# The second of four dense products of an attention and feed-forward kernel, recast as seven block products

## The chip, the cores and the metric

The kernel runs on one core of a Trainium2 chip. The core has TensorE (PE, matrix products; its weight loads are a row of their own, PEld), VectorE (DVE), ScalarE (ACT), GpSimd (POOL) and SyncE (SP). SP and POOL also issue transfers, which 16 DMA engines carry out; POOL issues the ones that add to what stands at the destination. Work data lie in SBUF (128 partitions), matmul results in PSUM (8 banks, a bank holding 128 x 512 fp32). Each engine runs its own list of instructions in order, and waits where an operand or a buffer is not ready. The metric is device microseconds of one execution; the median of several runs counts.

## The reference

Two sequences (B = 2) of 448 tokens (S), 12 heads of 64. First capped attention:

```python
scores = scale * np.matmul(q, k.transpose(0, 1, 3, 2))
scores = cap * np.tanh(scores / cap)
...
attn = attn / (np.sum(attn, axis=-1, keepdims=True) + 1e-09)
return np.matmul(attn, v).astype(np.float32)
```

Its 896 x 768 result goes through two feed-forward stages, each of two dense products (768 to 2048 and 2048 to 768), the first with `g = h * np.cos(h)`, the second with `g = h * (1.0 / (1.0 + np.exp(-h)))`:

```python
h = x @ w_in
g = h * np.cos(h)
return (g @ w_out).astype(np.float32)
```

So there are four dense products: in 1, out 1, in 2, out 2.

## The kernel before, in words

**Precision.** Every fp32 operand of a dense product is split into a high and a low fp32r part; a product of two is three matmuls (high x high, high x low, low x high, `three`). All matmuls have 448 columns. The split of a tile is one copy on ACT (high part) and one subtraction on DVE (low part): `split`. Weights arrive as 64-bit words and are turned into fp32 by two instructions on ACT and two on DVE (`convert`); some of the early ones by one on ACT and three on DVE (`w_abs`, `w_bits`).

**Attention** (to L437) runs pair by pair of heads, its order written out by hand.

**In 1** (`gemm_in`, L542) runs over 16 chunks of the 2048 features, its order also written out by hand. For each chunk TensorE does 36 matmuls (6 blocks of 128 x 3 x 2 sequences). `cos_unit` (L518) computes h cos h with ACT and DVE and at once splits g into `gh` and `gl`, which stay in SBUF until out 1 has read them.

**Out 1** (`gemm_out`, L828) is a plain product: 6 output blocks x 2 sequences x 16 chunks x 3 = 576 matmuls. Its weights come in 18 pieces of 5 or 6 blocks (`cuts`), each converted, split and used once for each sequence. Behind each output block stand the combinations T1 to T4 which in 2 needs.

**In 2** (`gemm_sums`, L898) and **out 2** (`gemm_last`, L1030) are already computed as seven block products each: the operands are cut in 2 x 2 blocks, and seven products of block sums replace the eight of the plain way. That is 504 matmuls each. In in 2 the sums of weight blocks (`sums`) are made on DVE for the first four of eight block rows (p = 0 to 3), and by accumulating transfers for the other four (L913). In out 2 the weight sums are accumulating transfers (`gather`, L1052), and the sums of g run on DVE (`sum_g`).

**The scheduler.** Out 1, in 2 and out 2 are lists of tasks (`do`, with a cost, the buffers that it reads and writes, and a due time). `run_plan` (L653) places them before the kernel is built, each engine taking the ready task with the earliest deadline for which the buffers are free; what comes out is a fixed order of instructions for each engine. Buffers are few: a ring of 8 tiles for split weights, 5 double tiles, 8 PSUM banks, and some 37 half tiles of 128 x 896.

Of the kernel before, what the change touches and what calls it, by code (L numbers as in the profile page):

```python
# [38 lines left out]
def tile_attention_ffn_ffn(  # L39
# [72 lines left out]
    cuts = [(0, 6), (6, 11), (11, KF)]  # L112
    wjobs = []
    for w_in, w_out in ((w_in1, w_out1), (w_in2, w_out2)):
        wi, wo = w_in.bitcast(I32), w_out.bitcast(I32)
        for n in range(KF):
            fc = n if w_out is w_out1 else n // 2 + n % 2 * HP
            wjobs.append((KD, wi[fc]))
        if w_out is w_out1:
            for dm in range(KD):  # L120
                for k0, k1 in cuts:
                    wjobs.append((k1 - k0, wo[dm][:, 2 * P * k0:2 * P * k1]))
        else:
            for n in range(4 * (HK + 1)):
                wjobs.append((KD, wo[n]))
# [63 lines left out]
    with ExitStack() as actx:  # L189
# [144 lines left out]
        def recip(p):  # L334
# [6 lines left out]
            eng = nc.sync if p < NPT - 1 else nc.scalar  # L341
            eng.dma_start(d.rearrange("h (a n) -> (h a) n", a=16), s[:, 0])
            r = ap2.tile([P, S], F32, tag="rb", name=f"rb{p}", bufs=4)
            for u in range(2):
                eng.dma_start(r[u * D:(u + 1) * D, :], d[1 - u:2 - u].to_broadcast([D, S]))
            rb[p] = r

        def norm_mul(p):
            if p < 0:
                return  # L350
            nc.vector.tensor_tensor(out=rb[p], in0=xu.pop(p), in1=rb[p], op=ALU.mult)
# [83 lines left out]
        for p in range(NPT - 2, NPT):  # L435
            norm_mul(p)
            norm_split(p)  # L437
# [4 lines left out]
    ps_ctx = ctx.enter_context(ExitStack())  # L442
    ps = ps_ctx.enter_context(tc.tile_pool(name="ps", bufs=1, space=PSUM, reuse_waits="tile"))
# [3 lines left out]
    g = []  # L447

    def more_g(n):
        for fc in range(len(g), n):  # L450
            if fc < ND:
                t = Part(f"g{fc}", F32R, doubles)
                g.append((t.view(0), t.view(1), (t,)))
            else:
                t = [Part(f"g{x}{fc}") for x in "hl"]
                g.append((t[0].view(), t[1].view(), t))

    def drop_g(fc):
        for t in g[fc][2]:
            t.drop()  # L460

    more_g(GL)
    t_slots = [(tpool, f"t{n}") for n in range(3)]
    halves += t_slots
    rt = [Part(f"r{n}", F32) for n in range(3)]
    pbank = [ps.tile([P, B, 512], F32, name=f"ps{n}") for n in range(4)]
    count = {"ps": 0, "r": 0}

    def finish():
# [3 lines left out]
        more_g(KF)  # L473

    def ps_tile():
        count["ps"] += 1
        return pbank[(count["ps"] - 1) % 4]

    def r_tmp():
        count["r"] += 1  # L480
        return rt[(count["r"] - 1) % 3].view()

    def mm3(pt, wi, rhs, first, last):
        ops = []
        for i, (rh, rl) in rhs:
            hi, lo = whi[wi][:, i], wlo[wi][:, i]
            ops += [(hi, rh), (hi, rl), (lo, rh)]
        for m, (l, r) in enumerate(ops):
            nc.tensor.matmul(pt, l, r, start=first and m == 0, stop=last and m == len(ops) - 1)  # L489

    def xr(kk, b):
        return [(i, (xt[i][b].view()[:, 0, :], xt[i][b].view()[:, 1, :])) for i in kk]

    def cut(pieces):
        r = r_tmp()
        views, at = [], 0
        for h, fc, bs in pieces:
            n = bs.stop - bs.start
            views.append((h, r[:, at:at + n, :], g[fc][0][:, bs, :], g[fc][1][:, bs, :]))
            at += n  # L500
        return views

    left = []

    def rest():
        while left:
            r, gh, gl = left.pop(0)
            nc.vector.tensor_tensor(out=gl, in0=r, in1=gh.bitcast(F32), op=ALU.subtract)

    def w_do(f, ws, *a):  # L510
        for wi in ws:
            f(wi, *a)

    def w_next(ws):
        if ws:
            w_abs(ws[-1] + 1)

    def cos_unit(pieces, ws):  # L518
        pieces = cut(pieces)
        for h, r, gh, gl in pieces:  # L520
            nc.scalar.activation(out=r.bitcast(I32), in_=h, func=AF.Copy, scale=1.0 / (2.0 * math.pi))
        w_do(w_bits, ws, 0)
        for h, r, gh, gl in pieces:
            nc.vector.scalar_tensor_tensor(out=r, in0=h, scalar=1.0 / (2.0 * math.pi), in1=r.bitcast(I32),
                                           op0=ALU.mult, op1=ALU.subtract)
        for h, r, gh, gl in pieces:
            nc.scalar.activation(out=r, in_=r, func=AF.Sin, scale=math.pi)
        w_next(ws)
        for h, r, gh, gl in pieces:
            nc.scalar.activation(out=r, in_=r, func=AF.Square)  # L530
        w_do(w_bits, ws, 1)
        w_do(w_bits, ws, 2)
        w_do(w_hi, ws)
        rest()
        for h, r, gh, gl in pieces:
            nc.vector.scalar_tensor_tensor(out=r, in0=r, scalar=-0.5, in1=h, op0=ALU.add, op1=ALU.mult)
        w_do(w_lo, ws)
        for h, r, gh, gl in pieces:
            nc.scalar.activation(out=gh, in_=r, func=AF.Copy)
            left.append((r, gh, gl))  # L540

    def gemm_in(base, unit, mid):  # L542
        half = [slice(0, 1), slice(1, 2)]
        both = slice(0, 2)
        kc = KD - 2
        pt = [ps_tile() for b in range(B)]
        w_load(base + 3)
        for b in range(B):
            for fc in range(2):
                mm3(pt[b][:, fc, :S], base + fc, xr(range(KD if b == 0 else kc), b), True, b == 0)  # L550
            if b == 0:
                mid()
                unit([(pt[b][:, fc:fc + 1, :S], fc, half[b]) for fc in range(2)], [base + 3])
        for fc in range(2):
            mm3(pt[1][:, fc, :S], base + fc, xr(range(kc, KD), 1), False, True)
            w_done(base + fc)
        todo = [(pt[1][:, fc:fc + 1, :S], fc, half[1]) for fc in range(2)]
        w_load(base + 4)
        for fc in range(2, KF):
            w_load(base + fc + 3)  # L560
            p = ps_tile()
            unit(todo, [base + fc + 2])
            for b in range(B):
                mm3(p[:, b, :S], base + fc, xr(range(KD), b), True, True)
            w_done(base + fc)
            todo = [(p[:, :, :S], fc, both)]
        w_load(base + KF + 3)
        unit(todo, [base + KF + 2])
        rest()
        for t in rt + [t for ts in xt for t in ts]:  # L570
            t.drop()
# [17 lines left out]
    LAT = {"PE": 280, "ACT": 210, "DVE": 170, "SP": 3500, "POOL": 4500}  # L589
    stock = {"ring": room, "bank": [], "half": halves, "dbl": doubles, "one": [], "raw": []}  # L590

    def do(eng, cost, fn, r=(), w=(), due=1e9, moves=0, lag=0):
        t = Task(eng, cost, (2000 + moves + lag) if moves else LAT[eng], fn, due)
        t.moves, t.lag = moves, lag
        for v in r:
            if v.writer:
                t.after.add(v.writer)
# [23 lines left out]
    def dve(n, fn, r, w, one=False, **k):  # L621
        do("DVE", 1.03 * (95 + (0.521 if one else 1.0417) * n), fn, r, w, **k)
# [592 lines left out]
```

## Time and profile before

| | |
|---|---|
| median of 3 runs | 541.18 us (541.01 to 541.87) |
| profiled execution | 541.54 us |
| its span, first to last instruction | 539.6 us |
| PE busy | 529.7 us (98%), 2772 matmuls |
| DVE busy | 408.5 us (76%), 542 instructions |
| ACT busy | 370.8 us (69%), 470 instructions |
| granted TensorE clock | 1.00 throughout |

The profiled execution is 1.94 us longer than its span, and 0.36 us above the median. A busy PE says that matmuls overlap without a gap, not that nothing could be taken away; how far the other engines are from holding PE up must be read stage by stage. A row of a stretch (view of windows) gives, from left to right: from and to, the length, busy time and number of instructions of PE, PEld, DVE, ACT and POOL, then the granted clock, the mean busy share of the DMA engines, and GB/s. A row of a group gives line, engine, operation, tiles and shapes, count, then busy time, mean ns of one, and idle time ahead of it. A row of the timeline gives start, length, and what ran.

### The profile page before, as it was taken

To read this page: it belongs to the slowest core of one execution; us is meant where nothing else is said; L and a number is where in the kernel's file an instruction comes from. 1 tells how busy PE (TensorE), PEld (TensorE's weight loads), DVE (VectorE), ACT (ScalarE), POOL (GpSimd) and SP (SyncE) were. 2 spreads that over 40 slices of the span, in tenths; PEclk is the share of its full clock that TensorE was granted. 3 is DMA by queue.
4 is the path that set the end of the run, shared out by engine and by line. 5 is a ranking of instruction groups with operands and counts; after the bars stand their busy time and mean duration, and the time that the engine had idled before them with its cause. 6 is when DMAs were issued, how large, how long until landed. Compare 5 with 4: busy or idle time off the path is not lost.

```text
span 539.6 us, 7350 instructions
## 1 busy us (share of the span) xinstructions
PE 529.7 (98%) x2772; PEld 445.4 (83%) x2772; DVE 408.5 (76%) x542; ACT 370.8 (69%) x470; POOL 59.2 (11%) x82
## 2 busy tenths in 40 slices
PE   8999999999999999999999999999999999999997
PEld 5444443999999999999999999999978899999996
DVE  4479997699888988776677698998569676955660
ACT  6989996387667777676676666888767555555531
POOL 0244442000000000000000000011221110420000
PEclk9999999999999999999999999999999999999999
DMA  8156453133333323697888650577798681892111
GB/s 297 55 143 199 137 178 112 35 118 117 118 117 118 114 73 95 211 321 240 269 265 288 230 174 2 183 239 213 228 263 234 177 219 27 175 262 57 52 51 52
DMA packets 26119, 87.15 MB, mean 161 GB/s; under 512 B 4376, under 2 KB 10052, under 8 KB 26084
## 3 DMA queue, kind: packets, MB, share of 16 engines
q1 hardware_dynamic: 18416, 67.51, 37.2%
q0 software_dynamic: 7104, 18.62, 15.5%
q10 hardware_dynamic: 564, 0.55, 0.4%
q8 instruction: 22, 0.36, 0.3%
q14 instruction: 13, 0.11, 0.1%
HBM read 71.18 MB, written 9.09 MB: 149 GB/s over the span
## 4 chain that ended last, share of the span: by engine, by line
PE 94%; ACT 3%; issue 1%; DVE 1%; DVEq 0%
PE bank L821 58%; PE ps L489 22%; PE po L293 5%; PE sc L259 4%; PE sm L311 2%; PE sc L263 2%; PE po L303 2%; ACT e L271 1%; PE warm L366 1%; ACT e L277 1%; DVE v L746 1%; ACT v L743 0%; ACT v L953 0%; ACT hl L743 0%; DVE e L319 0%
## 5 line engine op out<-in xcount | busy, mean ns | idle before, releaser
L821 PE MATMUL bank<-v,hl 128*128 128x448 f32 x828 | 170.2, 366 | 2.4 <-DVE hl L746 1.3
L821 PEld LDWEIGHTS bank<-v,hl 128*128 128x128 f32 x828 | 155.2, 188 | 15.8 <-DVE hl L746 1.9
L489 PE MATMUL ps<-x,hl 128*128 128x448 f32 x576 | 117.0, 365 | 0.0
L489 PEld LDWEIGHTS ps<-x,hl 128*128 128x128 f32 x576 | 108.1, 188 | 9.2 <-DVE xs L330 0.7
L821 PE MATMUL bank<-gh,hl 128*128 128x448 f32 x288 | 83.9, 366 | 0.0
L746 DVE TENSOR_TENSOR v<-v,v 128x896 fp32r<-128x896 f32 (+3 forms) x56 | 53.6, 969 | 30.1 <-ACT v L743 29.7
L743 ACT ACTIVATE v<-v 128x896 fp32r<-128x896 f32 (+2 forms) x48 | 39.9, 838 | 38.3 <-PE bank L821 29.6
L821 PEld LDWEIGHTS bank<-gh,hl 128*128 128x128 f32 x288 | 54.1, 188 | 4.4
L778 DVE SCALAR_TENSOR_TENSOR wraw<-wraw 128x768 int32<-128x768 int32 (+1 forms) x46 | 42.5, 927 | 15.4 <-ACT wraw L775 15.3
L775 ACT ACTIVATE wraw<-wraw 128x768 int32<-128x768 uint8 (+1 forms) x46 | 40.7, 889 | 18.5 <-DMA wraw<-in_moe_w_out 17.2
L821 PE MATMUL bank<-gl,hl 128*128 128x448 f32 x144 | 52.6, 365 | 0.0
L746 DVE TENSOR_TENSOR hl<-v,hl 128x768 fp32r<-128x768 f32 (+1 forms) x48 | 42.7, 894 | 9.2 <-ACT hl L743 8.6
L913 POOL DMA_DIRECT2D v<-v x16 | 14.0, 897 | 315.6 <-DVE v L784 264.4
L781 ACT ACTIVATE wraw<-wraw 128x768 f32<-128x768 f32 (+1 forms) x46 | 40.8, 889 | 7.8 <-DVE wraw L778 7.7
L271 ACT ACTIVATE e<-sc,scap 128x896 f32<-128x896 f32 (+1 forms) x48 | 40.1, 912 | 6.8 <-PE sc L259 6.7
L743 ACT ACTIVATE hl<-v 128x768 fp32r<-128x768 f32 (+1 forms) x48 | 37.2, 788 | 8.9 <-PE bank L821 6.5
L743 ACT ACTIVATE v<-bank 128x448 f32<-128x448 f32 (+2 forms) x43 | 22.7, 536 | 27.2 <-PE bank L821 25.7
L821 PE MATMUL bank<-v,v 128*128 128x448 f32 x180 | 38.6, 367 | 0.6 <-DVE v L746 0.6
L821 PEld LDWEIGHTS bank<-v,v 128*128 128x128 f32 x180 | 33.6, 188 | 3.9 <-DVE v L746 1.0
L277 ACT ACTIVATE e<-e,capt 128x3136 f32<-128x3136 f32 (+2 forms) x13 | 35.2, 2710 | 0.4
L784 DVE SCALAR_TENSOR_TENSOR wx<-wraw 128x768 int32<-128x768 int32 (+1 forms) x32 | 29.2, 914 | 6.3 <-ACT wraw L781 5.7
L821 PE MATMUL bank<-g,hl 128*128 128x448 f32 x144 | 31.2, 365 | 0.0
(84 smaller groups left out, 670.5 us busy)
## 6 DMA issues: line engine op xcount, KB each, us to landing
wraw<-in_moe_w_in SPq DMA_DIRECT2D x29, 768.0 KB, 4.3
wraw<-in_moe_w_out SPq DMA_DIRECT2D x22, 768.0 KB, 5.3
wraw<-in_moe_w_out SPq DMA_DIRECT2D x12, 640.0 KB, 4.4
wd<-wx SPq DMA_DIRECT2D x16, 384.0 KB, 2.6
v<-wd SPq DMA_DIRECT2D x16, 384.0 KB, 4.9
raw<-in_qkv POOLq DMA_DIRECT2D x9, 480.0 KB, 4.6
v<-v POOLq DMA_DIRECT2D x16, 192.0 KB, 5.3
v<-wd POOLq DMA_DIRECT2D x8, 384.0 KB, 6.8
```

Source lines behind the costliest of these rows:

```text
L259: nc.tensor.matmul(ps[:, u, :S], kk[rows, cols], qq[rows, :S], start=m == 0, stop=m == 2)
L271: nc.scalar.activation(out=e32[p][:, 2 * t:2 * t + n, :], in_=sc.pop((p, t))[:, :n, :S], func=AF.Tanh, scale=scap)
L277: nc.scalar.activation(out=e, in_=e, func=AF.Exp, scale=capt)
L293: nc.tensor.matmul(po[u * D:(u + 1) * D], vf[p][:, 2 * t + u, :], e32[p][:, 2 * t + u, :], start=first and n == 0, stop=last and n == len( ...
L489: nc.tensor.matmul(pt, l, r, start=first and m == 0, stop=last and m == len(ops) - 1)
L743: nc.scalar.activation(out=out, in_=src, func=AF.Copy, scale=scale)
L746: nc.vector.tensor_tensor(out=out, in0=a, in1=b, op=op)
L775: nc.scalar.activation(out=b[:, :, 0], in_=b.bitcast(U8)[:, :, 3], func=AF.Copy, scale=1.0 / 32, bias=-0.5 + 1.0 / 64)
L778: nc.vector.scalar_tensor_tensor(out=w(0), in0=w(1), scalar=-0x80000000, in1=w(0), op0=ALU.bitwise_and, op1=ALU.bitwise_or)
L781: nc.scalar.activation(out=w(1).bitcast(F32), in_=w(1).bitcast(F32), func=AF.Abs, scale=2.0 ** -112)
L784: nc.vector.scalar_tensor_tensor(out=view(), in0=w(1), scalar=3, in1=w(0), op0=ALU.logical_shift_left, op1=ALU.bitwise_or)
L821: nc.tensor.matmul(bank, x, y, start=first and m == 0, stop=last and m == len(ops) - 1, skip_group_check=True)
```

## The change

Out 1 becomes seven block products of 72 matmuls (504 instead of 576), each over 4 pieces q of weights and of g. For this the host lays out `w_out` of the first stage as that of the second already is, so the weights come in 16 pieces of 6 blocks instead of 18. The pieces live in half tiles, sums are formed from them in place: the list `WE` names the engine for the four sums of weights (all by accumulating transfers, 16 of 384 KB), `GE` for the four sums of g (DVE for three, transfers of 448 KB for the third). g is no longer split in in 1: it is kept whole and split (`split_g`) for each product anew, as the weights are (`split_w`). One weight block, x22, is written to DRAM and read back. The outputs of out 1 are combined from the seven products on DVE.

In 1 becomes a list of tasks too, so that the scheduler orders it together with the rest; its units are 448 columns wide (`unit`), and its weights use `convert`. The last two normalisations of attention become tasks (their quotients go through SP's queue instead of ACT's).

In in 2 the sums of weights run on DVE for six block rows and by transfers for two (`S3E`). In out 2 two of the four sums of weights move from transfers to DVE (`LE`). The due times of the early conversions of the last weights (`DUE`) are later.

```diff
+    def plus(eng, kb, o, a, b, r, w):
+        if eng == "DMA":
+            dma("POOL", kb, lambda: nc.gpsimd.dma_start(o(), b(), accum_op=ALU.add), r, w, adds=True)
+        else:
+            dve(kb * 2, lambda: sub_(o(), a(), b(), ALU.add), r, w)
...
+    GE, WE, LE = [["DVE", "DMA"][n] for n in (0, 0, 1, 0)], [["DVE", "DMA"][n] for n in (1, 1, 1, 1)], [["DVE", "DMA"][n] for n in (0, 0)]
+    FE = "DVE"
+    S3E = [["DVE", "DMA"][n] for n in (0, 1, 1, 0, 0, 0, 0, 0)]
...
+        def unit(fc, b, pt):
+            t, subs = y_in(f"B{fc // HP + 1}{b + 1}", fc % HP // 2, gx)
...
+            act(S, lambda: copy(r().bitcast(I32), h(), 1.0 / (2.0 * math.pi)), [pt], w)
...
+            act(S, lambda: nc.scalar.activation(out=r(), in_=r(), func=AF.Sin, scale=math.pi), [table], w)
+            act(S, lambda: nc.scalar.activation(out=r(), in_=r(), func=AF.Square), [], w)
+            dve(S, lambda: nc.vector.scalar_tensor_tensor(out=r(), in0=r(), scalar=-0.5, in1=h(), op0=ALU.add, op1=ALU.mult), [pt], w, due=clock["pe"] + 5000)
...
+    def product(acc, key, w, d, gname, neg=False):
...
+        for q in range(NQ):
+            whi_, wlo_, flat = split_w(w[q])
+            v, ghi, glo = split_g(d, gname, q, neg)
...
+        x11 = fresh("11")
+        product(acc, "A", x11, gx, "B11")
...
+        x12 = fresh("12")
+        product(acc, "B", x12, gx, "B21", True)
+        sum_g(GE[0], gx, "B11", "B11", "B12")
...
+        for q in range(NQ):
+            w_sum(WE[0], y[q], y[q], x21[q])
+        product(acc, "C", y, gx, "B11")
...
+        sum_g(GE[1], gx, "B11", "B11", "B22")
+        for q in range(NQ):
+            w_sum(WE[1], y[q], y[q], x11[q])
+        product(acc, "A", y, gx, "B11", True)
...
+        for q in range(NQ):
+            w_sum(WE[2], x11[q], x11[q], x21[q])
+        sum_g(GE[2], gx, "B12", "B22", "B12")
+        product(acc, "A", x11, gx, "B12")
...
+        for q in range(NQ):
+            w_sum(WE[3], x12[q], x12[q], y[q])
+        product(acc, "C", x12, gx, "B22")
...
+        sum_g(GE[3], gx, "B21", "B11", "B21")
+        product(acc, "A", x22, gx, "B21")
...
-                    if p > 3:
-                        dma("POOL", 192, lambda o=o, y=y: nc.gpsimd.dma_start(flat(*o), flat(*y), accum_op=ALU.add), [sub[y]], [sub[o]], adds=True)
-                    else:
-                        dve(HK * P, lambda o=o, y=y: sub_(flat(*o), flat(*o), flat(*y), ALU.add), [sub[y]], [sub[o]])
+                    plus(S3E[p], 192, lambda o=o: flat(*o), lambda o=o: flat(*o), lambda y=y: flat(*y), [sub[y]], [sub[o]])
```

**VectorE in out 1.** Before, a piece of weights was converted into `wx` and split once (`hl` are the ring's tiles), and the rest were combinations of 448 columns:

```order
L778 SCALAR_TENSOR_TENSOR wraw_2195<-wraw_2195 128x768
L778 SCALAR_TENSOR_TENSOR wraw_2223<-wraw_2223 128x768
L784 SCALAR_TENSOR_TENSOR wx<-wraw_2195 128x768
L778 SCALAR_TENSOR_TENSOR wraw_2252<-wraw_2252 128x768
L784 SCALAR_TENSOR_TENSOR wx<-wraw_2223 128x768
L746 TENSOR_TENSOR hl_83<-wx,hl_82 128x768
L784 SCALAR_TENSOR_TENSOR wx<-wraw_2252 128x768
```

Now, ahead of the third product, the conversions go on, and splits of weights (`hl`), splits of g and sums of g (`v`, 896 wide) stand between them:

```order
L633 TENSOR_TENSOR v_2200<-v_1110,v_2200 128x896
L633 TENSOR_TENSOR hl_81<-v_1872,hl_80 128x768
L671 SCALAR_TENSOR_TENSOR v_2219<-wraw_2144 128x768
L633 TENSOR_TENSOR v_1110<-v_1110,v_1620 128x896
L633 TENSOR_TENSOR v_2228<-v_1234,v_2228 128x896
L633 TENSOR_TENSOR hl_84<-v_1960,hl_82 128x768
L633 TENSOR_TENSOR v_1234<-v_1234,v_1744 128x896
L665 SCALAR_TENSOR_TENSOR wraw_2169<-wraw_2169 128x768
L633 TENSOR_TENSOR v_2258<-v_1359,v_2258 128x896
```

Each of the four pieces of a product now asks DVE for one 768-wide and one 896-wide instruction, and each sum of g on DVE for a further one of 896.

**POOL.** Before, the queue went from the last transfers of attention (`sums`) straight to the sums of in 2 (L913); out 1 had no row there. Now these stand ahead of in 2's (v are half tiles of g, 896 wide, and of weights, 768 wide):

```order
L326 DMA sums_971<-xs_970 32x1x28 x2
L497 DMA v_1180<-v_1620 128x896
L497 DMA v_1265<-v_1744 128x896
L497 DMA v_1386<-v_1870 128x896
L497 DMA v_1872<-v_1972 128x768
L497 DMA v_1508<-v_1998 128x896
L497 DMA v_1960<-v_2133 128x768
L497 DMA v_2035<-v_2179 128x768
L497 DMA v_1872<-v_1655 128x768
L497 DMA v_2157<-v_2219 128x768
```

The 20 new accumulating transfers of out 1 begin here; the weight tile v_1872 gets its first addend in the fifth of these rows and its second in the ninth.

**VectorE where in 2 ends.** Before, the last block row (v_3359) was split without a sum on DVE ahead of it, since its sums were transfers:

```order
L746 TENSOR_TENSOR hl_80<-v_3258,hl_83 128x768
L746 TENSOR_TENSOR hl_84<-v_3359,hl_85 128x768
L746 TENSOR_TENSOR v_3550<-v_3097,v_3550 128x896
L746 TENSOR_TENSOR v_3097<-v_3097,v_3149 128x896
L746 TENSOR_TENSOR v_3149<-v_3195,v_3149 128x896
L746 TENSOR_TENSOR v_3586<-bank_1923,v_3481 128x448
L746 TENSOR_TENSOR v_3615<-bank_1925,v_3481 128x448
L746 TENSOR_TENSOR hl_83<-v_3258,hl_83 128x384
L746 TENSOR_TENSOR hl_80<-v_3359,hl_80 128x384
```

Now (v_3507 is that block row, of which four 384-wide sums stand a few rows ahead of these; the last row, which reads bank_1044 with v_3697, must be done before the last nine matmuls of in 2 may write this bank):

```order
L633 TENSOR_TENSOR v_3678<-bank_1041,v_3566 128x448
L633 TENSOR_TENSOR hl_80<-v_3406,hl_80 128x384
L633 TENSOR_TENSOR hl_85<-v_3507,hl_85 128x384
L633 TENSOR_TENSOR hl_86<-v_3507,hl_84 128x768
L671 SCALAR_TENSOR_TENSOR wx<-wraw_3568 128x768
L633 TENSOR_TENSOR v_3702<-v_3379,v_3702 128x896
L665 SCALAR_TENSOR_TENSOR wraw_3630<-wraw_3630 128x768
L633 TENSOR_TENSOR hl_83<-v_3658,hl_82 128x768
L633 TENSOR_TENSOR v_3739<-v_3599,v_3739 128x896
L671 SCALAR_TENSOR_TENSOR wx<-wraw_3630 128x768
L633 TENSOR_TENSOR v_3091<-v_3091,v_3252 128x896
L633 TENSOR_TENSOR v_3678<-bank_1044,v_3697 128x448
```

The sums of the block row, conversions of out 2's weights and out 2's first splits now all stand in DVE's list ahead of that row. Counted from the end of attention's quotients, these rows ahead of it are 183 of 768 elements, 124 of 448, 46 of 896 and 32 of 384; TensorE's list has 1,575 matmuls of the dense products ahead of the nine.

## Rows read from the trace of the kernel before

**Rows 1.** The page: span, and busy time of each engine.

```profile
span 539.6 us, 7350 instructions
PE 529.7 (98%) x2772; PEld 445.4 (83%) x2772; DVE 408.5 (76%) x542; ACT 370.8 (69%) x470; POOL 59.2 (11%) x82
```

**Rows 2.** The chain in order of time: start, us, what.

```profile
93.75 116.93 PE ps L489 x576
210.68 187.96 PE bank L821 x926
...
405.23 16.37 PE bank L821 x79
...
426.88 109.37 PE bank L821 x538
...
536.65 0.39 DVE v L1152
```

**Rows 3.** Groups of PE by line: the matmuls of out 1.

```profile
L821 PE MATMUL bank<-gh,hl 128*128 128x448 f32 x288 | 83.9, 366 | 0.0
...
L821 PE MATMUL bank<-gl,hl 128*128 128x448 f32 x144 | 52.6, 365 | 0.0
...
L821 PE MATMUL bank<-g,hl 128*128 128x448 f32 x144 | 31.2, 365 | 0.0
```

**Rows 4.** Windows over the end of in 2 and the start of out 2.

```profile
386.10:400.70 14.60, 13.45 (x66) 11.89 (x65) 8.91 (x12) 9.95 (x16) 2.64 (x3) 1.00 0.77 223
400.70:415.30 14.60, 14.02 (x67) 12.30 (x68) 14.08 (x18) 13.74 (x22) 3.48 (x4) 1.00 0.84 213
415.30:429.90 14.60, 13.34 (x67) 11.99 (x66) 10.42 (x14) 8.04 (x13) 2.62 (x3) 1.00 0.66 196
```

**Rows 5.** Groups of DVE by line, shapes apart.

```profile
L746 DVE TENSOR_TENSOR hl<-v,hl 128x768 fp32r<-128x768 f32 x41 | 39.0, 952 | 4.9 <-ACT hl L743 4.2 <-issue 0.4 <-PE bank L821 0.2
...
L746 DVE TENSOR_TENSOR v<-v,v 128x896 fp32r<-128x896 f32 x28 | 30.5, 1090 | 27.0 <-ACT v L743 26.7
...
L746 DVE TENSOR_TENSOR v<-bank,v 128x448 f32<-128x448 f32 x22 | 13.5, 620 | 7.0 <-PE bank L821 6.9
...
L746 DVE TENSOR_TENSOR v<-v 128x384 f32<-128x384 f32 x12 | 6.6, 551 | 0.0
```

**Rows 6.** Timeline of DVE, where it works without a pause.

```profile
341.92 0.95 DVE L784 SCALAR_TENSOR_TENSOR v<-wraw 128x768 int32<-128x768 int32 x1
342.79 0.95 DVE L778 SCALAR_TENSOR_TENSOR wraw<-wraw 128x768 int32<-128x768 int32 x1
343.66 0.55 DVE L746 TENSOR_TENSOR v<-v 128x384 f32<-128x384 f32 x1
```

**Rows 7.** The window around it, DVE's densest stretch.

```profile
326.80:359.18 32.38, 32.38 (x162) 29.95 (x161) 31.34 (x47) 26.23 (x43) 0.98 (x1) 1.00 0.40 128
```

**Rows 8.** Timeline of DVE: its last row of attention's quotients.

```profile
96.65 0.32 DVE L339 RECIPROCAL sums<-sums 32x28 f32<-32x28 f32 x1
```

**Rows 9.** Waits: who waited for whom; us in total, times, longest.

```profile
DVE v L746 <- ACT v L743: 31.4, 24, 2.1
...
DVE wraw L778 <- ACT wraw L775: 15.3, 18, 3.1
...
DVE hl L746 <- ACT hl L743: 10.7, 9, 4.1
```

**Rows 10.** DMA queues: the page's, then those of 456 to 488 us.

```profile
q1 hardware_dynamic: 18416, 67.51, 37.2%
...
q0 software_dynamic: 1618, 4.44, 75.0%
...
v<-v POOLq DMA_DIRECT2D x8, 384.0 KB, 9.5
```

**Rows 11.** Groups of POOL by line: accumulating transfers.

```profile
L913 POOL DMA_DIRECT2D v<-v x16 | 14.0, 897 | 315.6 <-DVE v L784 264.4 <-DVE hl L746 24.2 <-DMA v<-v 18.9
...
L1052 POOL DMA_DIRECT2D v<-v x8 | 8.5, 1059 | 21.9 <-DVE hl L746 21.6 <-issue 0.3
```

More of the change, by code (lines that the diff above doesn't have):

```diff
@@ L472, in finish @@
         halves.extend((gpool2, f"gr{n}") for n in range(2 * (KF - GL)))
[L473 to L571, printed above, removed]
@@ L672, in run_plan @@
         events = [(0, -1, None)] + [(x, -1, None) for x in busy.values()]
+        started, line = [], 0
         for t in tasks:
             t.wait = len(t.after)
-            if not t.wait:
+            if t.eng == "X":
+                t.start = 0
+                started.append(t)
+                events.append((t.cost, t.n, t))
+            elif not t.wait:
                 ready[t.eng].append(t)
-        started, line = [], 0
         events.sort()
@@ L695, in run_plan @@
             for e in LAT:
-                if busy[e] > now:
+                if busy[e] > now or e == "EW":
                     continue
-                for t in sorted(ready[e], key=lambda t: (t.dl, t.n)):
+                for t in sorted(ready[e] + (ready["EW"] if e in ("POOL", "DVE") else []), key=lambda t: (t.dl, t.n)):
                     want = [v for v in t.vals if not v.held]
@@ new lines, in half_w, with w_sum, split_w, split_g @@
+    def half_w(v):
+        return v.buf.rearrange("p b s -> p (b s)")[:, :KMAX * P]
+    def w_sum(eng, o, a, b):
+        plus(eng, 384, lambda: half_w(o), lambda: half_w(a), lambda: half_w(b), [x for x in (a, b) if x is not o], [o])
+    def split_w(v):
+        hi, lo = Val("ring"), Val("ring")
+        flat = lambda t: t.buf.rearrange("p k f -> p (k f)")
+        split(KMAX * P, hi, lo, lambda: flat(hi), lambda: flat(lo), lambda: half_w(v), [v])
+        return hi, lo, flat
+    def split_g(d, name, q, neg):
+        t, subs = d[name, q]
+        v = Val("dbl", F32R)
+        hi, lo = v.sub(), v.sub()
+        h = lambda x: v.buf[:, x * B * S:(x + 1) * B * S]
+        split(B * S, hi, lo, lambda: h(0), lambda: h(1), lambda: t.buf.rearrange("p b s -> p (b s)"), subs, neg)
+        return v, hi, lo
@@ L1115, in gemm_last @@
         x11 = [fetch("11", q) for q in range(NQ)]
-        product("A", x11, "B11", lambda q: sum_g(("B11", q), ("B11", q), ("B12", q), sub_))
+        first = lambda w: [v for v, _ in w]
+        product(acc, "A", first(x11), gf, "B11")
+        sum_g(FE, gf, "B11", "B11", "B12", ALU.subtract)
         acc["B"] = [Val("bank") for d in range(HK)]
@@ L1120, in gemm_last @@
         x12 = [fetch("12", q) for q in range(NQ)]
-        product("B", x12, "B21")
+        product(acc, "B", first(x12), gf, "B21")
         for d in range(HK):
@@ L1130, in gemm_last @@
         for q in range(NQ):
-            gather(y[q], x11[q][1], x11[q][0])
-        product("A", y, "B11")
+            w_sum(LE[0], y[q][0], y[q][0], x11[q][0])
+        product(acc, "A", first(y), gf, "B11", True)
         for d in range(HK):
@@ L1141, in gemm_last @@
         for q in range(NQ):
-            gather(x12[q], y[q][1], y[q][0])
-        product("C", x12, "B22")
+            w_sum(LE[1], x12[q][0], x12[q][0], y[q][0])
+        product(acc, "C", first(x12), gf, "B22")
         for d in range(HK):
@@ L1146, in gemm_last @@
         x22 = [fetch("22", q) for q in range(NQ)]
-        for q in range(NQ):
-            sum_g(("B21", q), ("B21", q), ("B11", q), lambda o, a, b: neg_sub(o, a, b))
-        product("A", x22, "B21")
+        sum_g(FE, gf, "B21", "B11", "B21", ALU.subtract)
+        product(acc, "A", first(x22), gf, "B21")
         for d in range(HK):
```

340 lines of the change are left out of this document (179 added, 161 removed).

## Prediction

> **What bounds the kernel now.** I read the page first: TensorE is busy for 529.7 of 539.6 us, VectorE for 408.5, ScalarE for 370.8 [rows 1]. A reader should take from this only that TensorE is nowhere without work for long. The chain in order of time says it more sharply: from 93.75 us on it runs through matmuls alone, 576 in in 1 (116.93 us), then out 1, in 2 and out 2, and leaves TensorE only around 399 to 405, 422 to 427 and after the last matmul [rows 2]. The chain's 116.93 us for 576 give 0.2030 us for each matmul of 448 columns. From 93.75 to the end of the last chain piece of matmuls (426.88 + 109.37 = 536.25) are 442.5 us; the 2,160 matmuls of the four dense products need 2,160 x 0.2030 = 438.5 of them. So TensorE stands still for only 4.0 us, and the windows show where: 1.15, 0.58 and 1.26 us are missing from its busy time in the three stretches in which in 2 ends and out 2 begins [rows 4]. Taking matmuls away is therefore worth their full 0.2030 us each, as long as the other engines feed the rest on time. That second half decides this change.
>
> **What is taken away.** Out 1's matmuls are 288 + 144 + 144 = 576 [rows 3]; seven products of 72 are 504. That is 72 x 0.2030 = 14.6 us less on the path. Without any stall the profiled execution would be 541.54 - 14.6 - 4.0 = 522.9 us; attention ahead of 93.75 and the tail behind the last matmul keep their instructions but for two small quotients, and I leave them as they are.
>
> **What is added to VectorE.** I price its rows by the groups: 0.952 us for 768 elements, 1.090 for 896, 0.620 for 448, 0.551 for 384 [rows 5]. A product needs four splits of weights and four of g, 4 x (0.952 + 1.090) = 8.2 us, so seven need 57.2. The 16 conversions, two rows each, are 32 x 0.952 = 30.5. Splits and combinations of the blocks that come out are 21 + 18 rows of 448, 24.2. Twelve sums of g on VectorE are 12 x 1.090 = 13.1. Out 1 thus asks VectorE for 125 us, while TensorE takes 504 x 0.2030 = 102.3. In exchange g is no longer split in in 1 (16 x 1.090 = 17.4 us gone), so part of the conversions can be made there, as far as half tiles are free to keep them. In 2 gets two more block rows of sums, 8 x 0.551 = 4.4 us.
>
> Whether that is too much shows in the order: at the end of in 2 the last nine matmuls wait for a VectorE row that has 183 rows of 768, 124 of 448, 46 of 896 and 32 of 384 ahead of it since attention's last quotient. At the prices above that is 174.2 + 76.9 + 50.1 + 17.6 = 319 us. VectorE is free for it from 96.65 + 0.32 = 97.0 us [rows 8]; TensorE, without a stall, comes to that point at 93.75 + 1,575 x 0.2030 = 413.5. So 319 us of rows stand in 316.5 us of time. Before the change VectorE's load never came near that for long.
>
> **How long those rows really take.** This is the disputed cost, and I bound it from both sides. Where VectorE works without a pause, instructions that last 0.95 us start 0.87 apart, the next before the last has ended [rows 6]; that is 0.915 of the sum of their durations. In its densest stretch, 47 instructions in 32.38 us, it kept on like this with only 1.04 us of pauses [rows 7]. At that rate the 319 us take 292. At the other end, if each row needs the result of the one ahead, nothing overlaps, and they take 319. I take the middle, 305, since the new rows are of both kinds: splits that are independent of each other, and combinations that read what the row ahead wrote.
>
> To it come waits. The largest of VectorE's waits for ScalarE were 31.4 + 15.3 + 10.7 = 57.4 us over the whole kernel [rows 9]. Most of it was harmless, since VectorE was ahead. I take a third, 19 us, as what a loaded VectorE still loses, an estimate without a row of its own. 305 + 19 = 324 us against 316.5 makes VectorE 7 to 8 us late at the end of in 2. TensorE loses this in pieces wherever the rows bunch: in the first two products of out 1, and in the second half of in 2. Out 2 asks less, and I add 0.5 us for it. **Stalls: 8 us** in place of 4.0, which are in this figure, as they lie at the same place.
>
> The Trainium skill, page "VectorE: DVE Perf Modes", section "The DRAIN you can't avoid", says that a VectorE instruction doesn't start until the pipeline of the one ahead is empty. By that rule nothing overlaps, and the sum would go by 319 us and not 305. The 0.87 us between starts of 0.95 us speak against it here.
>
> **Transfers.** 20 accumulating transfers are new in out 1. In the stretch of before in which 12 of 384 KB ran, their queue took 75.0% of 32 us, so 2.0 us of all engines each [rows 10]; 16 of 384 KB and 4 of 448 are 41 us. A load of 768 KB takes 37.2% of 539.6 us / 67.51 MB x 0.786 MB = 2.3 us. The order puts some nine loads, nine smaller transfers of half that size and 15 of the accumulating ones against the first four products, 21 + 10 + 30 = 61 us of queue in 58.5 us. That is full, but each product's sums are issued about a product (14.6 us) ahead of their use, and one took 9.5 us to land in the full stretch of before. I cost them at nothing; the cover is that lead. The issue on POOL (0.9 to 1.1 us each [rows 11]) lies on an otherwise idle queue.
>
> **The sum.** 541.54 - 14.6 - 4.0 + 8 = 530.9 us for an execution like the profiled one; that one is 0.36 us above the median, so **530.6 us**.
>
> **Rivals.**
> *Nothing new is waited for.* If the rows overlap as in the densest stretch, 292 us and 19 of waits are 311 in 316.5, and only stalls like those of before remain, 0 to 4 us: 522.5 to 526.5. For it: VectorE kept 96% busy (31.34 of 32.38) there while TensorE lost nothing [rows 7]. Against it: there it lived off a lead, and here the load lasts for 200 us.
> *VectorE becomes the bound.* No overlap, 319 + 19 = 338 us, 21.5 late: 522.5 + 22 = 544.5, slower than before. For it: many of the new combinations are chains. Against it: rows 6. By the skill's rule this is what would happen.
> *The block sums come late.* Products 3 to 6 of out 1 each wait for four transfers. If the full queue makes each set 5 us late behind its lead, that is 4 x 5 = 20 us: 526.5 + 20 = 546.5, slower. It ends on the other side from 4 us a set on (542.5). For it: 61 us of transfers in 58.5. Against it: the lead, and the queue is nearly empty from the fifth product on.
> *Something between*, sets 2 to 3 us late or waits of half of the 57 us: 534.5 to 540.1.
>
> **Chances.** The forecast, 527 to 534.5: 0.55. Nothing new waited for: 0.20. Something between: 0.10. Within 0.2% (540.1 to 542.3, about what a measurement of this kernel can tell from no change): 0.04. VectorE the bound 0.04, late sums 0.07. So faster 0.85, same 0.04, slower 0.11. The range 523 to 539.5 leaves out these 0.15, and some 0.04 at the edges of the cases beside them.
>
> **What would show it.** Right: 2,700 matmuls on the page; matmuls still 0.203 us apart in the chain; VectorE's busy time 30 to 45 us higher; the chain leaving TensorE for VectorE rows of splits and combinations in out 1 and in 2, with 6 to 10 us of stalls in sum, most of them before 414 us. Wrong: the chain passing through accumulating transfers in out 1 (late sums), VectorE busy without pause and TensorE idle by 15 us or more (no overlap), or stalls in in 1, where I expect none: its weights now pass through two ScalarE and two VectorE rows and narrower units, and its start waits for the last normalisations, for which 12.2 us of matmuls (60) are the cover.

## The result and the profile after

The new kernel takes **526.43 us** (median of 4 runs, 525.39 to 527.83) against 541.52 for the kernel before beside it: a ratio of 0.9722 (95% interval 0.9693 to 0.9752), 15.1 us faster. The forecast was 530.6. The profiled execution took 525.39 us.

The page of the new kernel, to be read against [rows 1]:

```profile
span 523.6 us, 7364 instructions
PE 515.9 (99%) x2700; PEld 431.8 (82%) x2700; DVE 446.2 (85%) x604; ACT 404.7 (77%) x551; POOL 63.0 (12%) x86
```

72 matmuls are gone, and VectorE has 37.7 us more to do. The chain in order of time (start, us, what) shows how little TensorE waits. It begins with an accumulating transfer of in 2 at 343.85 us, runs through ScalarE and VectorE to 350.00, and from there through matmuls alone, where before it left them twice on its way [rows 2]:

```profile
343.85 4.18 DMA v<-v
...
348.11 0.85 ACT v L630
...
348.99 0.97 DVE v L633
...
350.00 170.05 PE bank L708 x826
```

The windows, one for each dense stage (in 1, out 1, in 2, out 2; columns as in [rows 4]):

```profile
93.11:209.96 116.85, 116.85 (x579) 108.48 (x578) 105.80 (x149) 101.65 (x162) 3.59 (x4) 1.00 0.58 187
209.96:312.10 102.14, 102.14 (x506) 94.82 (x504) 95.26 (x116) 80.69 (x112) 15.77 (x18) 1.00 0.74 204
312.10:415.72 103.62, 103.24 (x506) 94.47 (x504) 96.01 (x133) 88.43 (x138) 5.25 (x6) 1.00 0.71 234
415.72:519.67 103.95, 103.95 (x504) 94.47 (x503) 76.85 (x83) 52.12 (x68) 7.02 (x8) 1.00 0.38 109
```

Two things can be seen here. In out 1, where stalls were forecast, TensorE works 102.14 of 102.14 us beside a VectorE that works 95.26; in in 2 only 0.38 us are missing. And out 2 has no pause either, yet its 504 matmuls take 103.95 us, 0.2063 each, where before it was 109.37 / 538 = 0.2033 [rows 2] and in out 1 it is 102.14 / 504 = 0.2027.

The disputed stretch is from 97.0 us to the end of in 2. Its window, and the groups of VectorE in it, answer to [rows 7] and [rows 5]:

```profile
97.00:413.40 316.40, 316.02 (x1556) 292.01 (x1555) 291.72 (x386) 266.73 (x407) 24.61 (x28) 1.00 0.68 208
```

```profile
L633 DVE TENSOR_TENSOR hl<-v,hl 128x768 fp32r<-128x768 f32 x43 | 40.8, 952 | 0.2
...
L633 DVE TENSOR_TENSOR v<-v,v 128x896 fp32r<-128x896 f32 x24 | 26.1, 1087 | 1.7 <-ACT v L630 1.5
...
L633 DVE TENSOR_TENSOR v<-bank,v 128x448 f32<-128x448 f32 x24 | 14.6, 620 | 3.0 <-PE bank L708 2.8
```

The 29 groups of that list add up to 316.3 us for 386 instructions, at the same durations as before; VectorE was busy with them for only 291.72 us, 0.922 of the sum, and paused for 24.7. The largest waits that ended those pauses (against [rows 9]; us in all, times, longest):

```profile
DVE v L633 <- ACT v L630: 4.3, 6, 1.6
DVE v L771 <- ACT v L770: 3.5, 6, 1.5
DVE v L636 <- ACT v L630: 3.4, 2, 3.1
DVE v L633 <- PE bank L708: 2.8, 5, 1.1
```

### The profile page after: what moved, and what is told of

Its sections match the earlier page's. It is cut to its first block, busy times and chain, and to the rows that moved or that the text cites. A ratio compares the mean times of both kernels' runs of the same rounds, so it can differ in the third digit from the quotient of the medians.

```text
span 523.6 us, 7364 instructions
## 1 busy us (share of the span) xinstructions
PE 515.9 (99%) x2700; PEld 431.8 (82%) x2700; DVE 446.2 (85%) x604; ACT 404.7 (77%) x551; POOL 63.0 (12%) x86
## 2 busy tenths in 40 slices
DMA packets 27559, 93.69 MB, mean 179 GB/s; under 512 B 4536, under 2 KB 9188, under 8 KB 27524
## 5 line engine op out<-in xcount | busy, mean ns | idle before, releaser
L708 PE MATMUL bank<-v,hl 128*128 128x448 f32 x1332 | 274.7, 367 | 0.1
L708 PEld LDWEIGHTS bank<-v,hl 128*128 128x128 f32 x1332 | 250.2, 188 | 22.4 <-DVE hl L633 0.4
L633 DVE TENSOR_TENSOR v<-v,v 128x896 fp32r<-128x896 f32 (+4 forms) x103 | 100.6, 998 | 19.4 <-ACT v L630 19.1
L708 PE MATMUL bank<-x,hl 128*128 128x448 f32 x576 | 117.0, 366 | 0.0
L708 PEld LDWEIGHTS bank<-x,hl 128*128 128x128 f32 x576 | 108.3, 188 | 9.0 <-DVE xs L324 0.7
L630 ACT ACTIVATE v<-v 128x896 fp32r<-128x896 f32 (+2 forms) x82 | 69.4, 857 | 50.3 <-PE bank L708 37.9
L665 DVE SCALAR_TENSOR_TENSOR wraw<-wraw 128x768 int32<-128x768 int32 x60 | 57.0, 954 | 2.7 <-ACT wraw L662 2.5
L662 ACT ACTIVATE wraw<-wraw 128x768 int32<-128x768 uint8 x60 | 54.7, 912 | 5.3 <-DMA wraw<-in_moe_w_out 4.1
L668 ACT ACTIVATE wraw<-wraw 128x768 f32<-128x768 f32 x60 | 54.1, 910 | 2.9 <-DVE wraw L665 2.7
L497 POOL DMA_DIRECT2D v<-v x28 | 24.6, 951 | 230.2 <-DVE v L771 106.7
L287 PE MATMUL po<-e,vf 128*64 128x448 f32 x144 | 29.4, 541 | 0.6 <-ACT e L271 0.6
## 6 DMA issues: line engine op xcount, KB each, us to landing
v<-v POOLq DMA_DIRECT2D x16, 384.0 KB, 11.6
```

Source lines behind the costliest of these rows:

```text
L287: nc.tensor.matmul(po[u * D:(u + 1) * D], vf[p][:, 2 * t + u, :], e32[p][:, 2 * t + u, :], start=first and n == 0, stop=last and n == len( ...
L497: dma("POOL", kb, lambda: nc.gpsimd.dma_start(o(), b(), accum_op=ALU.add), r, w, adds=True)
L630: nc.scalar.activation(out=out, in_=src, func=AF.Copy, scale=scale)
L633: nc.vector.tensor_tensor(out=out, in0=a, in1=b, op=op)
L662: nc.scalar.activation(out=b[:, :, 0], in_=b.bitcast(U8)[:, :, 3], func=AF.Copy, scale=1.0 / 32, bias=-0.5 + 1.0 / 64)
L665: nc.vector.scalar_tensor_tensor(out=w(0), in0=w(1), scalar=-0x80000000, in1=w(0), op0=ALU.bitwise_and, op1=ALU.bitwise_or)
```

## The experiments

All start from the new kernel except where said. Times are medians of four runs; each set was run beside the kernel before (541.2 to 541.7 us). What a part costs or gives is the difference to 526.43. The new kernel's own four executions lie 2.4 us apart (525.39 to 527.83), so a difference of 1 or 2 us says little by itself.

### How much room VectorE has

The subtraction that makes the low part of g is repeated (it writes the same values) in out 1: for every second piece, then for all. No other instruction moves.

```diff
-        dve(n, lambda: (neg_sub if neg else sub_)(vlo(), ...), [hi, *r], [lo])
+        dve(n, lambda: [(neg_sub if neg else sub_)(vlo(), ...) for _ in range(again)], [hi, *r], [lo])
...
-    split(B * S, hi, lo, ..., subs, neg)
+    split(B * S, hi, lo, ..., subs, neg, 2 if d is gx and q % 2 else 1)   # second run: 2 if d is gx else 1
```

> Every second low-part subtraction of g in out 1 is done twice (14 more VectorE rows of 128x896, the same values written again), all orders otherwise those of the new kernel. In the new kernel VectorE is busy 95.3 of the 102.1 us of out 1, so 6.9 us are pauses. Theory, VectorE is just below the bound and its pauses are a true reserve: 14 rows of about 0.97 us are 13.6 us, less 6.9 of pauses, so 5 to 8 us slower than the new kernel (531.5 to 534.5 us), with stalls of TensorE in out 1 and the start of in 2. Rival, its order is so tight that every us shows: 13 to 14 us slower (539.5). Rival, it has a lead of many us and the bound is far: under 2 us slower (below 528.5).

> All 28 low-part subtractions of g in out 1 are done twice (28 more VectorE rows of 128x896, about 27 us), nothing else moved. Theory, pauses of 6.9 us are the reserve: 27 - 7 = 20 us, less up to 4 us if pauses of in 2 take some back: 16 to 20 us slower than the new kernel (542 to 547 us). Rival, every us shows: 27 us (553). Rival, a lead of many us: under 8 us (below 534).

Measured: **533.19 us** with 14 (ratio to before 0.9848, 0.9833 to 0.9863) and **547.09** with 28 (1.0105, 1.0076 to 1.0134). VectorE's busy time on the page rose by 14.7 and 29.3 us, the kernel's time by 6.8 and 20.7. So some 8 us were free, and every further microsecond cost about one. Both fell where the theory of a small reserve had put them (the second 0.1 us above its range). But waiting alone doesn't make this price. These are TensorE's waits for VectorE and ScalarE among its block products, first with 14, then with 28 (us in all, times, longest; the new kernel has one of 0.3):

```profile
PE bank L708 <- DVE hl L633: 3.1, 2, 1.9
PE bank L708 <- ACT bank L630: 1.1, 2, 0.8
```

```profile
PE bank L708 <- DVE hl L633: 9.8, 3, 4.2
PE bank L708 <- ACT bank L630: 2.9, 3, 1.7
PE bank L708 <- DVE v L633: 0.9, 2, 0.6
```

They are 4.2 of the 6.8 us and 13.6 of the 20.7. In the windows of the run with 14 (the two short ones around its first long stall) a second cost can be seen:

```profile
209.94:318.29 108.35, 105.11 (x505) 95.71 (x504) 106.24 (x125) 79.09 (x109) 15.77 (x18) 0.98 0.70 192
264.00:268.00 4.00, 2.08 (x11) 1.61 (x10) 4.00 (x5) 2.34 (x3) 0.00 (x0) 0.99 1.07 271
268.00:272.00 4.00, 4.00 (x14) 3.56 (x13) 3.96 (x5) 3.54 (x7) 0.00 (x0) 0.59 1.07 289
```

TensorE stood still for 1.9 of 4 us while VectorE worked 4.00 of 4.00. Behind that stall the granted clock is 0.59 for 4 us, mostly the lower of its two levels (1.00 is 2.4 GHz, 0.5 is 1.2 GHz), and only 14 matmuls pass, where full clock has 20. Such stretches of lower clock stand behind the longer stalls of the runs below too, and none is in the new kernel (clock 1.00 in all its windows).

### Whether TensorE is still the bound

The 72 matmuls of the fourth product of out 1 are left out. First the order stays as it was; in a second run the scheduler is told that they cost nothing.

```diff
-                    mms(banks[k].buf[:, :S], ops, fresh and q == 0, q == NQ - 1)
+                    if not (d is gx and neg and gname == "B11"):
+                        mms(banks[k].buf[:, :S], ops, fresh and q == 0, q == NQ - 1)
```

> The 72 matmuls of the fourth product of out 1 (the second that reads the first sum of weights with B11) are left out, so that the output lacks this product; its splits, sums and transfers stay. Theory, TensorE is the bound and VectorE close behind: out 1 would last 87.5 us with 95.3 us of VectorE rows in it, so 7 to 9 us of the 14.6 come back as stalls, in out 1 or up to the end of in 2: 517.5 to 520 us. Rival, TensorE alone is the bound: the full 14.6 us, 511 to 512.5 us. Rival, VectorE or the transfers already set the pace: less than 3 us faster (523.5 or more).

> Again without the 72 matmuls of the fourth product of out 1 (its result is missing in the output), but now the scheduler knows that they cost nothing, and orders the rest for it. Theory, the earlier run gained nothing because its fixed order had bank copies behind splits that wait for transfers, all planned for 14.6 us of matmuls that weren't there; ordered anew, VectorE's reserve of about 8 us is what can be won: 517 to 520 us. Rival, the transfers of out 1 can't come earlier whatever the order: 524 us or more. Rival, TensorE is the only bound: 511 to 513 us.

Measured: **527.11 us** (ratio 0.9742, 0.9725 to 0.976), and **529.78** ordered anew (0.9781, 0.9742 to 0.9821). Nothing is won. TensorE waits at the start of the fifth product instead (waits of TensorE, then the chain, in the run with the old order):

```profile
PE bank L708 <- ACT v L630: 13.2, 1, 13.2
```

```profile
241.69 8.30 DMA v<-v
250.28 15.87 DMA v<-v
267.56 77.59 PE bank L708 x369
```

The theory of 7 to 9 us coming back was too hopeful, and the rivals with 523.5 and 524 us or more came true: 13.2 of the 14.6 came back in one wait, and the clock fell behind it. In the new order it is no better: 268.26 us in its chain for the start of the fifth product, behind a transfer of 12.87. With the matmuls in place TensorE comes there at 209.96 + 288 x 0.2027 = 268.3. So the transfers and the other engines are only just ahead of it. Which of them it is was asked by taking transfers out of the first of these kernels, again with the order kept: the four that sum g for the fifth product (`none` is set for them), then also the four that sum its weights.

```diff
-            dma("POOL", kb, lambda: nc.gpsimd.dma_start(o(), b(), accum_op=ALU.add), r, w, adds=True)
+            dma("POOL", kb, lambda: None if none else nc.gpsimd.dma_start(o(), b(), accum_op=ALU.add), r, w, adds=True)
```

> As the run without 72 matmuls in fixed order (527.1 us, a stall of 13.2 us ahead of the fifth product of out 1), and the four accumulating transfers of 448 KB that make the sum of g for the fifth product are left out too (that sum is not formed). Theory, these transfers end last ahead of the fifth product, so the stall there shrinks by 5 us or more: 519 to 522 us. Rival, the transfers of weights in the same queue end last: 525 to 528. Rival, rows of ScalarE and VectorE set the time there, not transfers: 525.5 to 528 here and in the next run.

> As the run before, and the four accumulating transfers of 384 KB that make the sum of weights for the fifth product are left out as well (neither sum is formed). Theory, with both sets gone nothing of a transfer ends late ahead of the fifth product; what is left is the time that ScalarE and VectorE need for rows planned there, some 9 us behind the start: 517 to 521 us. Rival, ScalarE's and VectorE's rows alone set the time: 525.5 to 528 us. Rival, TensorE alone: 511 to 513 us.

Measured: **525.98 us** (0.9725, 0.9691 to 0.9759) and **523.19** (0.9659, 0.9634 to 0.9684). Both missed the theory's range: the first lies in the ranges of both its rivals, the second between its theory and its first rival. The wait was 13.1 us without the four, and 9.8 us without the eight, so the transfers of weights had been as late as those of g. The windows of the second run show what was left:

```profile
239.00:254.00 15.00, 15.00 (x75) 13.72 (x74) 14.93 (x17) 11.37 (x16) 4.64 (x6) 1.00 1.07 243
254.00:264.00 10.00, 0.23 (x2) 0.05 (x1) 10.00 (x12) 9.73 (x14) 0.65 (x1) 0.73 1.04 303
```

While TensorE stands, VectorE works 10.00 of 10.00 us and ScalarE 9.73, so in this order, which was planned with the 72 matmuls in place, these rows hold the fifth product up by 9.8 us without any of the eight transfers. In the new kernel as it is, then, the transfers of out 1 come about 14.6 - 13.2 = 1.4 us early at this place, and VectorE with ScalarE about 14.6 - 9.8 = 4.8 us. This is an estimate: it takes it that nothing else moves when matmuls and transfers are left out. (The two can't be told apart here: both are full.)

### Which engine makes the sums

Three lists were changed by themselves; the scheduler orders anew each time. In out 1 all weight sums go to VectorE; in in 2 the sums are set back to the engines of before; in in 2 all go to VectorE.

```diff
-    WE = ... (1, 1, 1, 1)
+    WE = ... (0, 0, 0, 0)
...
-    S3E = ... (0, 1, 1, 0, 0, 0, 0, 0)
+    S3E = ... (0, 0, 0, 0, 1, 1, 1, 1)
...
-    S3E = ... (0, 1, 1, 0, 0, 0, 0, 0)
+    S3E = ... (0, 0, 0, 0, 0, 0, 0, 0)
```

> The 16 accumulating transfers of weights in out 1 become 16 rows of 128x768 on VectorE, about 0.9 us each, 14.4 us; the scheduler orders anew. Theory, VectorE has a reserve of about 8 us in and around out 1 (14 doubled subtractions cost 6.8 us, 28 cost 20.7): 14.4 - 8 = 5 to 8 us slower than the new kernel (531.5 to 534.5 us). Rival, the transfers are what keeps out 1 tight, and without them it gains as much room as VectorE loses: 525 to 528 us. Rival, a quarter of the rows bunches and stalls bring slow clock: more than 10 us slower (537 or more).

> The new kernel with only the engines of in 2's weight sums set back to what they were (VectorE for block rows 0 to 3, accumulating transfers for 4 to 7). Theory, the 4 us of stalls at the end of in 2 and the start of out 2 came from these late transfers and buffers that they hold: 2 to 4 us of stalls come back there and the short one at 347 us goes (527.5 to 530 us). Rival, the old stalls came from the order of the old list and are gone with it: within 1 us of the new kernel (525.5 to 527.5). Rival, relieving VectorE of 8 rows is worth more than the transfers cost: 1 us or more faster (525 or less).

> The 8 accumulating transfers that in 2 still has in the new kernel (block rows 1 and 2) become 8 rows of 128x384 on VectorE, about 0.5 us each, 4 us. Theory, the pauses of VectorE in in 2 (7.6 of 103.6 us) cover them, and the short stall at 347 us behind such a transfer goes: within 1 us of the new kernel, 525 to 527 us. Rival, the reserve is already spent ahead of in 2: 3 to 5 us slower (529 to 531). Rival, without the transfers the order gains elsewhere: 524 or less.

Measured: weight sums of out 1 on VectorE **538.41 us** (0.9943, 0.9928 to 0.9957); in 2 as before **545.12** (1.0078, 1.005 to 1.0105); in 2 all on VectorE **533.84** (0.9852, 0.9831 to 0.9873). All three are worse than the main theory had it: the first lies where its last rival stood (537 or more), the other two above every range that was given.

*Weight sums of out 1 on VectorE*, 12.0 us slower. The stall is where the work of out 1 ends and in 2 begins, with VectorE full (10.00 of 10.00 in the second stretch) and the clock down:

```profile
315.00:325.00 10.00, 4.43 (x15) 3.46 (x15) 9.93 (x19) 8.34 (x16) 0.06 (x1) 0.83 0.29 88
325.00:335.00 10.00, 9.37 (x32) 7.87 (x32) 10.00 (x15) 5.66 (x9) 1.73 (x2) 0.66 0.45 114
```

14.4 us of rows less a reserve of 8 would be 6.4, and in these two stretches TensorE stands still for 5.57 + 0.63 = 6.2. The low clock adds 4.3 (47 matmuls keep it busy for 13.80 us there, at 0.2027 they would for 9.5), and a longer pace of the matmuls to the end 0.9 (170.96 us for the last 826 in its chain, 170.05 in the new kernel).

*In 2 as before*, 18.7 us slower, and slower than the kernel before the change. Its chain goes through the accumulating transfers of in 2's last block rows:

```profile
354.46 6.80 DMA v<-v
361.55 8.20 DMA v<-v
379.44 7.70 DMA v<-v
389.36 4.90 DMA v<-v
394.78 8.17 DMA v<-v
```

Two windows, out 1 and in 2 of this run, show that the loss isn't in in 2 alone: they last 5.8 and 15.1 us longer than in the new kernel (102.14 and 103.62), though no row of out 1 changed its engine. The order of out 1 moved too.

```profile
209.97:317.94 107.97, 104.79 (x506) 95.91 (x505) 97.29 (x119) 80.45 (x114) 14.06 (x16) 0.98 0.65 179
317.94:436.69 118.75, 108.77 (x505) 96.12 (x504) 97.00 (x127) 89.07 (x137) 14.90 (x17) 0.97 0.81 247
```

So without this edit, as the scheduler then orders the rest, the seven products in out 1 would have been a loss of 3.6 us. *In 2 all on VectorE* lost 7.4 us, and its first stall isn't in in 2: the order of out 1 moved with it, and the fifth product waits for its sums again:

```profile
250.30 18.58 DMA v<-v
268.97 1.42 ACT v L630 x2
271.60 62.09 PE bank L708 x297
```

The lead of 1.4 us doesn't survive a small change of order. Whether the edit of in 2 is a gain in itself was tried on the kernel **before**:

```diff
-                    if p > 3:
+                    if p in (1, 2):
```

> The kernel before, with only the engines of in 2's weight sums changed as the new kernel has them (accumulating transfers for block rows 1 and 2, VectorE for all others). Theory, the 4 us of stalls that the kernel before had at the end of in 2 and the start of out 2 came from transfers of the last four block rows that ended late, and the change of these engines took them away: 537 to 538.5 us. Rival, the sums on VectorE make it late there, and stalls of the same size come from it: 541 to 543 us. Rival, the transfers of rows 1 and 2 come late at the start of in 2 instead: 545 us or more.

Measured: **547.64 us** (1.0116, 1.0093 to 1.0139), 6.4 us slower than the kernel before. The stalls at the end of in 2 were gone, as the theory had it, but a new one of 4.7 us stood at the start of in 2, with VectorE full and again a lower clock. The time is that of the third case, its reason is not: the chain goes through VectorE's rows there, not through transfers.

```profile
330.00:336.00 6.00, 1.25 (x6) 0.85 (x5) 6.00 (x10) 4.67 (x9) 1.74 (x2) 0.78 0.53 171
346.00:434.00 88.00, 88.00 (x430) 80.21 (x429) 75.97 (x100) 67.53 (x107) 1.94 (x3) 1.00 0.57 192
```

From 346 us on TensorE is never idle, and still its matmuls take 88.00 / 430 = 0.2047 us. This longer pace, which out 2 of the new kernel has too, was the last question.

### The longer pace in out 2

One matmul of 64 columns is put into TensorE's list, in a bank that the next matmul starts anew: ahead of out 2's first product, or ahead of its third.

```diff
+                    if d is gf and gname == "B11" and key == "A" and fresh and q == 0 and k == 0:   # third product: key == "C"
+                        x, y = ops[0]
+                        nc.tensor.matmul(banks[k].buf[:, :64], x, y[:, :64], start=True, stop=True, skip_group_check=True)
                     mms(banks[k].buf[:, :S], ops, fresh and q == 0, q == NQ - 1)
```

> One matmul of 64 columns is put ahead of the first of out 2 (its result is overwritten by the next). In the new kernel the matmuls of out 2 follow each other by 206.7 ns each without any stall, in all other stages by 202.7; in two runs the longer pace ended behind a short gap. Theory, the pace is a state of TensorE's pipeline that a disturbance can end: out 2 goes at 202.7 ns and the kernel is 2 us faster than the new one (523.4 to 524.5 in its shorter runs). Rival, the pace belongs to what out 2 reads and writes, or to a state that so short a matmul doesn't end: no change (525.4 to 527.8).

> The matmul of 64 columns now stands ahead of the third product of out 2 instead of the first. Theory, the longer pace is a state that begins before out 2 and lasts until something disturbs it: the first two products (144 matmuls) go at 206.7 ns, the last five (360) at 202.8, and the kernel is 360 x 0.004 = 1.4 us faster than the new one, some 0.6 us slower than the run with the short matmul at the start. Rival, the pace depends on how out 2's first product starts, or on what out 2 reads and writes: all of out 2 at 206.7 ns, and no gain.

Measured: **523.74 us** with it at the start (523.45 to 524.15; ratio 0.9672, 0.9656 to 0.9688), **524.02** at the third product (523.84 to 524.6; 0.9673, 0.9649 to 0.9697). The first is the fastest kernel of this study, 2.7 us below the new one, with intervals that do not overlap. The pace accounts for 1.7 of it (out 2 takes 102.23 us and not 103.95); against the two shorter executions of the new kernel (525.39 and 525.6) the median is 1.8 us lower. At the third product 0.6 us less than that was expected to be won, and 0.3 less was. The ends of the two chains:

```profile
415.87 0.03 PE bank L838
415.89 102.23 PE bank L708 x504
```

```profile
445.54 0.03 PE bank L838
445.57 73.05 PE bank L708 x360
```

102.23 / 504 = 0.2028 and 73.05 / 360 = 0.2029 us: behind the short matmul the pace is the short one. The window of 459.60 to 517.70 us, first of the new kernel and then of the one with the short matmul at the third product, shows it without modelled ends, by counting:

```profile
459.60:517.70 58.10, 58.10 (x283) 52.80 (x282) 35.33 (x40) 24.14 (x32) 0.00 (x0) 1.00 0.10 30
```

```profile
459.60:517.70 58.10, 58.10 (x289) 53.85 (x288) 35.04 (x40) 24.61 (x32) 0.00 (x0) 1.00 0.10 30
```

Six matmuls more in the same 58.10 us, at the same clock and with nearly the same work on the other engines.

## Why the prediction came out as it did

**The matmuls taken away: right.** 72 x 0.2030 = 14.6 us; out 1's 504 take 102.14 us without a pause.

**VectorE's rows: the step that was mis-sized.** The order's 319 us of rows were right (316.3 by the groups). "I take the middle, 305" was wrong: they took 291.72, the lower bound of 292. The densest stretch of before [rows 6, 7] gave the right price by itself, 0.915 of the sum where 0.922 was measured; that the figures agree to 0.3 us is in part luck, as the sum was 2.5 us too high. The upper bound's fear of dependent rows isn't empty. Of these three in the kernel before, the last two read what the row ahead wrote, and each starts 0.04 us after the end of that row:

```profile
94.82 0.62 DVE L351 TENSOR_TENSOR rb<-xu,rb 128x448 f32<-128x448 f32 x1
95.48 0.39 DVE L358 CAST x<-rb 128x448 fp32r<-128x448 f32 x1
95.91 0.63 DVE L359 TENSOR_TENSOR x<-rb,x 128x448 fp32r<-128x448 f32 x1
```

What the prediction had wrong is how often this happens. The rows of the new kernel overlap by 316.3 - 291.72 = 24.6 us; at 0.08 us each (0.95 against 0.87 [rows 6]) that is some 300 of the 386, an estimate. By the rule that the prediction took from the Trainium skill, "VectorE: DVE Perf Modes", section "The DRAIN you can't avoid", nothing overlaps; that would be 316 us here and disagrees with the 291.72. The same section adds that a next instruction that is not held starts earlier, which the prediction left out.

**The waits: about the size, but not a loss.** 19 us were taken, 24.7 us of pauses came. With 292 us of rows the prediction's own sum is 311 in 316.5, and VectorE is 5.5 us early instead of 7 to 8 late. The doubled subtractions found 8 us of room, the run without eight transfers 4.8 at its tightest place. So the rival "nothing new is waited for" came true, which had a chance of 0.20: 526.43 lies at the upper edge of its 522.5 to 526.5. The forecast's 527 to 534.5 missed by its stalls, and the wider range of 523 to 539.5 held because it took this rival in. That VectorE stands close to being the bound, the core of the argument, was right: 14.7 us more on it cost 6.8.

**The stalls.** Forecast 8 us; what came is 3.1. From the first matmul of in 1 to the last of out 2 are 350.00 + 170.05 - 93.11 = 426.9 us, and 2,088 x 0.2030 are 423.9. Some 1.6 of the 3.1 are out 2's longer pace (103.95 us for 504 matmuls, 102.3 at 0.2030), for which the prediction had no term, and 1.3 lie in in 2, of which TensorE stands still for 0.38. The stalls forecast in out 1's first two products didn't come, and the chain doesn't leave TensorE for VectorE's rows there. (The 4.0 of before were read too freely as well: the three stretches of [rows 4] show 3.0 of them.) With a start of in 1 0.6 us earlier (93.69 to 93.11) the account closes: 14.6 + 4.0 - 3.1 + 0.6 = 16.1 of the 16.15 us between the profiled executions.

**Transfers at nothing: right in the sum, wrong in its cover.** The queue was as full as reckoned:

```profile
224.60:239.20 14.60, 14.60 (x74) 13.55 (x73) 13.37 (x15) 11.46 (x16) 3.48 (x4) 1.00 1.03 296
239.20:253.80 14.60, 14.60 (x74) 13.56 (x73) 14.59 (x16) 10.21 (x14) 7.07 (x8) 1.00 1.07 242
253.80:268.40 14.60, 14.60 (x74) 13.55 (x73) 11.30 (x13) 10.89 (x15) 1.77 (x2) 1.00 1.07 290
```

A share of 1.03 to 1.07 for three products, and 11.6 us to landing on the page in place of 9.5 [rows 10]. "About a product ahead of their use" held when they were issued, but at the fifth product some 1.4 us were left of it. The prediction gave products 3 to 6 four transfers each; by the lists `WE` and `GE` the fifth waits for eight, four of weights and four of g, and it is the tightest place. The rival "the block sums come late" was nearer than its 0.07 tells.

**In 2's sums: costed at 4.4 us of VectorE, which misses what they do.** Setting them back costs 18.7 us, applying them alone to the kernel before costs 6.4. The prediction didn't ask what out 1's products would cost without this edit, and so couldn't see that the two belong together. Both figures include what the scheduler moved elsewhere.

**The rest** came as written: 2,700 matmuls, VectorE's busy time up by 37.7 us (30 to 45 forecast), no stall in in 1. Not settled: whether ScalarE or VectorE is the later one at the fifth product, and how much of the cost of in 2 all on VectorE is the low clock and how much the pace. The edits of in 1, of out 2's sums (`LE`) and of the due times (`DUE`) were not run by themselves.

## What to carry to other kernels

Price a loaded engine by the busy time that the trace shows in its densest stretch (here 0.92 of the sum of durations), look in the new order for rows that need the row right ahead of them, and count the engine's waits as a loss only where it has no lead. A full TensorE doesn't say how near the next bound is: doubling harmless instructions on one engine shows its lead, leaving out matmuls shows that of the others, and here three bounds lay within 8 us of each other. Read the waits beside the time, since a stall can bring a lower clock with it. Where a scheduler orders everything, a part of a change can cost 6 us alone and save 19 in company, so test each part both ways.

## What the runs showed of the hardware

TensorE has a longer pace without any pause: 0.2063 us for a matmul of 448 columns in out 2 in place of 0.2028, at a granted clock of 1.00, and with no wait of TensorE in it. In the new kernel it begins where in 2 ends, at about 415 us, with no wait of TensorE near it (28.8 us hold 143 matmuls ahead of 415.30 and 141 behind it); it lasts for the 504 matmuls of out 2, and one matmul of 64 columns ended it at both places where it was put. What starts it, and what in the pipeline differs, stays open. And behind the longer stalls the granted clock fell (0.59 in the 4 us behind a stall of 1.9 us, 0.66 in 10 us behind one of 5.6), so a stall cost more than its own length. The short stalls of the kernel before left it at 1.00 [rows 4].
